# V loaded one group earlier, between two output stores, and one query cast moved from ScalarE to GpSimd

## The chip, the cores and the metric

The kernel runs on one NeuronCore of a Trainium2 chip, as one launch. The metric is the device time of that launch in microseconds. Three runs of the kernel before took 281.1, 279.26 and 280.06 us, a median of 280.06 us. The core has five engines that run side by side: TensorE (PE, matrix products; PEld is its weight load), VectorE (DVE), ScalarE (ACT), GpSimd (POOL) and SyncE (SP), which here only issues DMAs.

## The reference

The computation is an attention with pooled keys and values, followed by a two-layer MLP. There are 8 batches of 8 heads, 576 tokens and a head width of 64.

```python
k_p = k.reshape(B, H, Sp, pool, D).mean(axis=3)      # pool = 8, Sp = 72
v_p = v.reshape(B, H, Sp, pool, D).mean(axis=3)
scores = scale * np.matmul(q, k_p.transpose(0, 1, 3, 2))
attn = softmax(scores)
attn_out = np.matmul(attn, v_p)
x = attn_out.transpose(0, 2, 1, 3).reshape(B * S, H * D)      # 4608 x 512
h = x @ w_in                                                 # 512 -> 2048
out = gelu_tanh(h) @ w_out                                   # 2048 -> 512
```

All inputs and the output are float32. Inside, the kernel works with bf16 operands and float32 sums.

## The kernel before

**Groups.** The 4608 tokens are worked on as nine groups of 512. Groups 0 to 7 take the first 512 tokens of their batch. Group 8, called R, collects the last 64 tokens of all eight batches. The order is `seq = [0, 1, 2, 3, 4, 5, 6, R, 7]`. `n_` counts the place in that order and `g` is the group. While the MLP of one group runs on TensorE, the attention of the next group is prepared on the other engines, and its few products are slipped in between those of the MLP.

**Order by hand.** The scheduler is switched off. The instructions of an engine run in the order in which the program emits them. The MLP of a group (`mlp`, line 536) is a chain of numbered steps, and `at(hooks, s, f, ...)` says that the function `f` is emitted just before step `s`. Steps 0 to 63 are the first layer, steps 64 to 175 are the second (seven products of 16 matmuls each). A step number fixes the place in each engine's queue. It does not fix a time: an engine that has nothing to wait for runs ahead of TensorE. SyncE does this often, and its queue is in order: a DMA whose data or buffer isn't ready holds back all that stand behind it.

**Groups 3 and later are "fast".** Their first layer is `hidden_fast` (line 462), where a part of the products is done with fewer multiplications, out of sums and differences of blocks. Its partial results are `k2`, `k0` and `k1`. `k2` and `k0` are written to two tiles with the tag `osb`, the same two buffers that hold the output rows of the group before until they are stored. Line 500 copies the first product into `k2`, in the buffer of the first store. Line 507 copies the sum `x4` into `k0`, in the buffer of the second. Each has to wait until the store that reads its buffer has landed. After line 507 the product with `S(3)`, at step 28, adds again onto `x4`. The matmuls of these products have line 474, the plain ones of the first layer line 383, those of the second layer line 586.

**Stores.** A group's output leaves in two stores of 512 KB (`store_pair`, line 412): the first after the product 3 (step 159), as soon as VectorE has finished `k0`, the second after the last product (step 175), as soon as ScalarE has copied `x`.

**Loads.** Keys and values of a batch share one tile `kv`, of which there are two buffers, so that batch b uses the buffer of batch b-2. `load_kv(n, parts)` (line 760) makes the tile and issues, on SyncE, the 1 MB of K and two halves of 128 KB (part 0) and the 1 MB of the main part of V (part 1). Lines 112, 107 and 105 are these DMAs; line 121 is the load of the queries (1 MB). Before the change, place `n_` loads the K and V of place `n_ + 2` in one go at step 28 (for `n_ = 1` in two parts, at steps 45 and 164). V of a later group is pooled on VectorE (line 149 and 151) at steps 148 and 161 of the group two places ahead of it, K at steps 5 and 17 of the group one place ahead.

**Transposes.** The cast queries `q_b`, the pooled keys and the exponentials are transposed by DMAs, which SyncE issues too: `qT` (line 232), `kTd` (line 211), `eT` (line 306).

**Query casts.** The queries of group 2 are cast to bf16 by `cast_q` (line 128) in four quarters on ScalarE, at steps 22, 26, 30 and 34 of group 1's MLP. The DMA transpose into `qT` stands at step 35, and the first scores (line 248) at step 68. The queries of later groups are cast by GpSimd.

Of the kernel before, what the change touches and what calls it, by code (L numbers as in the profile page):

```python
# [19 lines left out]
def kernel(  # L20
# [21 lines left out]
    nc = tc.nc  # L42
# [11 lines left out]
    seq = list(range(B - 1)) + [R, B - 1]  # L54
# [33 lines left out]
    st = [dict() for _ in range(B + 1)]  # L88
# [8 lines left out]
    def kv_tile(b):  # L97
        st[b]["kv"] = kvp.tile([128, NB, 8, D], F32, name="kv", tag="kv")
# [4 lines left out]
    def load_half(b, which, eng):  # L103
        if which == "v":
            eng.dma_start(out=st[b]["kv"][64:128, 4], in_=rows(v, b)[0:64])
        else:
            eng.dma_start(out=st[b]["kv"][0:64, 4], in_=rows(k, b)[512:576])

    def load_main(b, which, c0, c1, eng):
        t, w0, b0 = (k, 0, 0) if which == "k" else (v, 64, 5)  # L110
        src = rows(t, b)[w0 + 128 * c0:w0 + 128 * c1].rearrange("(c p) pl d -> p c pl d", p=128)
        eng.dma_start(out=st[b]["kv"][:, b0 + c0:b0 + c1], in_=src)
# [647 lines left out]
    def load_kv(n, parts=(0, 1)):  # L760
        if n != B - 1:
            b = B - 1 if n == R else n
            if 0 in parts:
                kv_tile(b)
                load_main(b, "k", 0, 4, nc.sync)
                load_half(b, "k", nc.sync)
                load_half(b, "v", nc.sync)
            if 1 in parts:
                load_main(b, "v", 0, 4, nc.sync)

    def at(hooks, s, f, *a):
        hooks.setdefault(s, []).append(lambda: f(*a))
# [6 lines left out]
    hooks = {}  # L779
# [46 lines left out]
    for n_, g in enumerate(seq):  # L826
        if n_ == 0:
            continue
        hooks = {}
        fast = n_ >= 3  # L830
        if n_ == 1:
            for i in range(1, 4):
                at(hooks, i, w_sums, i, 0, NP, nc.vector)
            at(hooks, 36, g_sums, 0, 4)
            at(hooks, 57, g_sums, 4, 6, (0,))
        elif fast:
            at(hooks, 41, g_sums, 0, 2, (0,))
            at(hooks, 57, g_sums, 2, 6, (0,))
            at(hooks, 65, g_sums, 6, 8, (0,))
            at(hooks, 65, g_sums, 0, 4, (1,))  # L840
        else:
            at(hooks, 20, g_sums, 0, 2)
            at(hooks, 36, g_sums, 2, 4)
            at(hooks, 57, g_sums, 4, 6, (0,))
        if not fast:
            at(hooks, 65, g_sums, 6, 8, (0,))
        at(hooks, 64 + 32, g_sums, 4, 8, (1,))
        if n_ + 1 < len(seq):
            n = seq[n_ + 1]
            b = B - 1 if n == R else n  # L850
            kv = n != B - 1
            if n_ == 1:
                for j in range(4):
                    at(hooks, 22 + 4 * j, cast_q, n, j, j + 1, nc.scalar)
                at(hooks, 35, qT_tile, n)
                at(hooks, 35, q_transpose_dma, n)
            if kv and not fast:
                t0 = 22 if n_ == 1 else 12
                at(hooks, t0, pool, b, 0, 5)
                at(hooks, t0, dup_k, b, 0, 5)  # L860
                at(hooks, t0, kT_tile, b, None)
                at(hooks, t0, k_transpose_dma, b)
                t1 = t0 + (16 if n_ == 1 else 24)
                at(hooks, t1, pool, b, 5, 9)
                at(hooks, t1, k_spread, b, [nc.gpsimd, nc.gpsimd])
                at(hooks, t1, spread_v, b, nc.gpsimd)
            elif kv:
                at(hooks, 5, pool, b, 0, 5, (0,))
                at(hooks, 17, pool, b, 0, 5, (1,))
                at(hooks, 17, dup_k, b, 0, 5)  # L870
                at(hooks, 17, kT_tile, b, None)
                at(hooks, 17, k_transpose_dma, b)
                at(hooks, 17, spread_gated, b)
                at(hooks, 40, k_spread, b, [nc.gpsimd, nc.gpsimd])
            if fast:
                at(hooks, 2, qT_tile, n)
                at(hooks, 2, q_transpose_dma, n)
            sc_at = [68, 68, 90, 90]
            for j in range(4):
                at(hooks, sc_at[j], scores, n, j)  # L880
                at(hooks, sc_at[j] + 1, exps, n, j)
            at(hooks, 80, eT_tile, n)
            for j in range(4):
                at(hooks, 80 if j < 2 else 92, norm, n, j, nc.vector if j > 1 else nc.gpsimd)
                at(hooks, 80 if j < 2 else 92, e_transpose_dma, n, j)
            at(hooks, 64 + 66, nc.scalar.preload_act_table_set, GELU_SET)
            at(hooks, 64 + 100, xT_tile, n)
            if n_ == 1:
                at(hooks, 64 + 100, values, n, (0,))
                at(hooks, 64 + 107, values, n, (1,))  # L890
            else:
                at(hooks, 64 + 104, values, n)
        if n_ + 2 < len(seq):
            n2 = seq[n_ + 2]
            s2 = 44 if n_ == 1 else 57
            for half, ahead in enumerate((3, 2)):
                if n_ + ahead < len(seq) and seq[n_ + ahead] == R:
                    if half == 0:
                        at(hooks, 9, q_tile, R)
                    at(hooks, 9, gate_queries, g)  # L900
                    at(hooks, 9, load_q, R, 2 * half, 2 * half + 2, nc.gpsimd)
            if n2 != R:
                at(hooks, s2, q_tile, n2)
                at(hooks, s2, load_q, n2, 0, 4, nc.sync)
            at(hooks, 64 + 52, cast_gated, n2)
            if n_ < 2:
                at(hooks, 64 + 100, qT_tile, n2)
                at(hooks, 64 + 100, q_transpose_dma, n2)
                at(hooks, 64 + 100, load_kv, n2, (1,))
            elif n2 != B - 1:  # L910
                b2 = B - 1 if n2 == R else n2
                at(hooks, 64 + 84, pool, b2, 5, 9, (0,))
                at(hooks, 64 + 97, pool, b2, 5, 9, (1,))
            if n_ == 1:
                at(hooks, 45, load_kv, n2, (0,))
            else:
                at(hooks, 28, load_kv, n2)
        mlp(g, hooks, n_ + 1 == len(seq), fast)


# [28 lines left out]
```

## Time and profile before

| | |
|---|---|
| median of three runs | 280.06 us (279.26 to 281.1) |
| the profiled execution | 278.7 us, its span 276.8 us |
| TensorE busy | 268.8 us, 97% |
| VectorE busy | 222.2 us, 80% |
| ScalarE busy | 176.3 us, 64% |
| GpSimd busy | 80.4 us, 29% |
| DMA traffic | 54.37 MB, 196 GB/s on the mean |
| granted TensorE clock | 1.0 throughout |

All times of the trace are counted from the start of the span. The span is the time from the first to the last instruction, and 1.9 us of the profiled execution lie outside it. In the page's second part each digit is the busy share of one fortieth of the span, in tenths, so 9 means 90% or more. In a timeline a row gives the start, the length, the engine, the line and the operation with its output and inputs; a bracket at its end gives how long the engine was idle before it and which instruction or DMA ended that. Matmuls overlap by a little, so that rows of TensorE can run into one another. The chain of waits goes back from the last instruction, at each step to what released it. A row of DMA issues gives how long the transfer took from its issue until it had landed.

The nine groups' MLPs start on TensorE at about 17.7 (group 0), 51.4, 80.2, 109.3, 136.8, 164.7, 192.3 (group 6), 220.5 (R) and 247.9 us (group 7).

### The profile page before, as it was taken

How to read it: one execution, taken by the hardware profiler on the slowest of the kernel's cores; microseconds unless marked ns; L12 is line 12 of the kernel's file. 1: busy time of each engine (PE TensorE's matmuls, PEld its weight loads, DVE VectorE, ACT ScalarE, POOL GpSimd, SP SyncE). 2: the span in 40 equal slices, each digit the busy share in tenths (PEclk: the TensorE clock that was granted, in tenths of full speed). 3: DMA queues.
4: the chain of work that ended last, by engine and by line, in shares of the span. 5: the costliest groups of instructions: out<-in, count | busy, mean ns of one | idle time of the engine just before them, and what ended most of it. 6: DMA issues, size and time to landing. Idle time of an engine off the chain costs nothing.

```text
span 276.8 us, 6558 instructions
## 1 busy us (share of the span) xinstructions
PE 268.8 (97%) x2668; PEld 192.5 (70%) x2686; DVE 222.2 (80%) x365; ACT 176.3 (64%) x265; POOL 80.4 (29%) x122
## 2 busy tenths in 40 slices
PE   8989999999999999999999999999999999999995
PEld 3668844445854588668866876688668966886684
DVE  5886869989966888989998989899989558955832
ACT  1586576579547764696469646964796469646820
POOL 4640282006420532224254425433224200300000
PEclk9999999999999999999999999999999999999999
DMA  7999999998999895899499979964742460253013
GB/s 229 310 195 280 362 385 241 294 366 204 248 215 248 267 278 137 176 300 247 121 216 286 285 134 216 245 184 123 178 154 54 119 152 2 48 117 87 1 41 114
DMA packets 67856, 54.37 MB, mean 196 GB/s; under 512 B 41458, under 2 KB 53746, under 8 KB 67826
## 3 DMA queue, kind: packets, MB, share of 16 engines
q1 hardware_dynamic: 65186, 50.67, 70.7%
q0 software_dynamic: 2496, 3.15, 6.1%
q8 instruction: 21, 0.34, 0.5%
q10 hardware_dynamic: 144, 0.13, 0.1%
q14 instruction: 9, 0.07, 0.1%
HBM read 36.70 MB, written 9.44 MB: 167 GB/s over the span
## 4 chain that ended last, share of the span: by engine, by line
PE 82%; DMA 6%; DVE 6%; ACT 2%; issue 1%; SPq 1%; DVEq 0%; ACTq 0%
PE mm L586 29%; PE mm L383 20%; PE c L474 12%; PE mm L399 5%; PE mm L394 5%; PE xo L344 3%; PE x L586 3%; DMA q_sb<-in_q_dram 2%; PE sc L248 2%; DMA qT<-q_b 2%; DVE den L264 1%; DMA eT<-eb 1%; PE mm L531 1%; DMA out_dram<-osb 1%; DVE eb L279 1%
## 5 line engine op out<-in xcount | busy, mean ns | idle before, releaser
L383 PE MATMUL mm<-xT,w_in_b 128*128 128x512 bf16 x290 | 68.4, 379 | 0.7
L586 PEld LDWEIGHTS <-gT 128*128 128x128 bf16 x512 | 48.3, 98 | 9.0 <-issue 1.4
L385 ACT ACTIVATE gT<-mm 128x512 bf16<-128x512 f32 x76 | 43.6, 599 | 14.3 <-PE mm L383 14.1
L383 PEld LDWEIGHTS <-w_in_b 128*128 128x128 bf16 x304 | 29.7, 98 | 31.0 <-issue 0.5
L586 PEld LDWEIGHTS <-stage 128*128 128x128 bf16 x384 | 37.6, 98 | 4.4
L92 ACT CAST xT<-xo 128x512 bf16<-128x512 f32 (+1 forms) x24 | 13.2, 610 | 28.5 <-PE xo L344 23.9
L586 PE MATMUL mm<-tw,gT 128*128 128x256 bf16 x240 | 30.0, 273 | 0.0
L586 PE MATMUL mm<-w_out_b,gT 128*128 128x256 bf16 x240 | 29.9, 273 | 0.0
L279 POOL TENSOR_TENSOR eb<-e,r 128x576 bf16<-128x576 f32 x14 | 15.8, 1150 | 46.2 <-DVE r L273 24.1
L264 DVE TENSOR_REDUCE den<-e 128x8 f32<-128x576 f32 x36 | 26.2, 729 | 2.9 <-ACT e L257 2.9
L257 ACT ACTIVATE e<-sc 128x576 f32<-128x576 f32 x36 | 22.4, 650 | 7.8 <-POOL eb L279 5.6
L586 PE MATMUL mm<-tw,stage 128*128 128x256 bf16 x224 | 26.7, 273 | 0.0
L92 ACT COPY osb<-mm 128x512 f32<-128x512 f32 x30 | 17.8, 593 | 14.0 <-PE mm L586 13.3
L149 DVE TENSOR_TENSOR kv<-kv 128x1024 f32<-128x1024 f32 (+3 forms) x19 | 23.2, 1220 | 3.8 <-DMA kv<-in_k_dram 2.6
L172 POOL TENSOR_TENSOR vbd<-kvb,vmask 128x256 bf16<-128x256 bf16 (+2 forms) x38 | 22.1, 605 | 5.6 <-DVE kvb L152 4.7
L474 PEld LDWEIGHTS <-ws 128*128 128x128 bf16 x192 | 18.8, 98 | 6.4 <-issue 0.5
L94 POOL CAST q_b<-q_sb 128x1024 bf16<-128x1024 f32 (+1 forms) x15 | 15.5, 1054 | 19.7 <-DMA q_sb<-in_q_dram 19.7
L474 PE MATMUL c<-tt,ws 128*128 128x256 bf16 x144 | 17.7, 272 | 0.1
L279 DVE TENSOR_TENSOR eb<-e,r 128x576 bf16<-128x576 f32 x18 | 17.1, 947 | 0.6
L434 DVE TENSOR_TENSOR stage<-gT 128x512 bf16<-128x512 bf16 (+1 forms) x25 | 13.7, 546 | 4.6 <-ACT gT L385 2.8
L94 POOL COPY kbd<-kTd 64x288 bf16<-64x288 bf16 x12 | 6.4, 533 | 35.0 <-DMA kTd<-kvb 34.7
L435 DVE TENSOR_TENSOR gT<-gT 128x512 bf16<-128x512 bf16 (+1 forms) x25 | 13.2, 528 | 3.4 <-ACT gT L385 1.2
(107 smaller groups left out, 423.6 us busy)
## 6 DMA issues: line engine op xcount, KB each, us to landing
kv<-in_k_dram SPq DMA_DIRECT2D x7, 1024.0 KB, 7.5
q_sb<-in_q_dram SPq DMA_DIRECT2D x7, 1024.0 KB, 9.9
kv<-in_v_dram SPq DMA_DIRECT2D x6, 1024.0 KB, 9.2
out_dram<-osb SPq DMA_DIRECT2D x12, 512.0 KB, 3.1
out_dram<-osb SPq DMA_DIRECT2D x11, 256.0 KB, 3.4
kv<-in_v_dram SPq DMA_DIRECT2D x4, 512.0 KB, 9.9
w_in_b<-in_moe_w_in_dram POOLq DMA_DIRECT2D x4, 512.0 KB, 6.8
w_out_s<-in_moe_w_out_dram SPq DMA_DIRECT2D x2, 1024.0 KB, 13.7
```

The source lines that it names most:

```text
L92: eng.copy(out=out, in_=in_)
L94: eng.tensor_copy(out=out, in_=in_)
L149: add(out=t[:, :, 0:4, :], in0=t[:, :, 0:4, :], in1=t[:, :, 4:8, :], op=ALU.add)
L172: eng.tensor_tensor(out=vbd[p0:128, b, n0:n1, :].rearrange("p (c r) (hh d) -> p c (r hh) d", c=max(m, 1), d=D), in0=kvb[p0:128, 4 + c0:4 + ...
L257: nc.scalar.activation(out=e.rearrange("p (x h) s -> p x (h s)", x=2), in_=sc[:, :, 0:4 * Sp], func=ACT.Exp, scale=1.0 / 64.0)
L264: nc.vector.reduce_sum(out=den, in_=e, axis=AX.X)
L279: eng.tensor_tensor(out=o.rearrange("p (pr hh s) -> p hh pr s", hh=2, s=Sp), in0=e.rearrange("p (hh pr) s -> p hh pr s", hh=2), in1=r.rear ...
L383: nc.tensor.matmul(out=hp, lhsT=w_in_b[:, ko, fo * 128:(fo + 1) * 128], rhs=st[g]["xT"][:, ko, :], start=(i == 0), stop=(i == KO - 1))
L385: nc.scalar.activation(out=gT[:, fo, :], in_=hp, func=ACT.Gelu_apprx_tanh)
L394: nc.tensor.matmul(out=hp[:, f, :], lhsT=w_in_b[:, ko, (fo + f) * 128:(fo + f + 1) * 128], rhs=st[g]["xT"][:, ko, c0:c0 + 256], start=(ko ...
L474: nc.tensor.matmul(out=acc[:, m, :], lhsT=lhs(i, m), rhs=rhs(i), start=bool(fresh and i == 0 and m % 2 == 0), stop=(i == 1), skip_group_ch ...
L586: nc.tensor.matmul(out=xs[p] if acc is xs else acc[:, p, :], lhsT=lt, rhs=rt, start=bool(fresh and m == 0 and (p == 0 or (last and acc is ...
```

## The change

Two things are moved.

First, V. In places `n_ = 2` and later, step 28 now loads only K and the two halves of place `n_ + 2`. The V of place `n_ + 3` is loaded at step 175 of place `n_`, between the first and the second output store. This happens at the ends of groups 2, 3 and 4, for the V of batches 5, 6 and 7. The V of batch 4, for which there is no earlier place, is loaded at step 14 of group 2, ahead of its K. As V can now be the first to use the tile, `load_kv` makes the tile when it isn't there yet.

Second, the last quarter of group 2's queries is cast by GpSimd at step 22. The other three stay on ScalarE at steps 22, 26 and 30.

```diff
     def load_kv(n, parts=(0, 1)):
         if n != B - 1:
             b = B - 1 if n == R else n
+            if "kv" not in st[b]:
+                kv_tile(b)
             if 0 in parts:
-                kv_tile(b)
                 load_main(b, "k", 0, 4, nc.sync)
                 load_half(b, "k", nc.sync)
                 load_half(b, "v", nc.sync)
...
             if n_ == 1:
                 for j in range(4):
-                    at(hooks, 22 + 4 * j, cast_q, n, j, j + 1, nc.scalar)
+                    at(hooks, 22 + 4 * (j % 3), cast_q, n, j, j + 1, nc.gpsimd if j == 3 else nc.scalar)
...
-            if n_ == 1:
-                at(hooks, 45, load_kv, n2, (0,))
-            else:
-                at(hooks, 28, load_kv, n2)
+            at(hooks, 45 if n_ == 1 else 28, load_kv, n2, (0,))
+            if n_ == 2:
+                at(hooks, 14, load_kv, n2, (1,))
+            if n_ > 1 and n_ + 3 < len(seq):
+                at(hooks, 64 + 111, load_kv, seq[n_ + 3], (1,))
         mlp(g, hooks, n_ + 1 == len(seq), fast)
```

## The prediction

> **What bounds the kernel now.** I read the page's busy times and slices first, then the chain of waits in order of time, then the timelines of the queues that the change touches.
>
> ```profile
> PE 268.8 (97%) x2668; PEld 192.5 (70%) x2686; DVE 222.2 (80%) x365; ACT 176.3 (64%) x265; POOL 80.4 (29%) x122
> PE   8989999999999999999999999999999999999995
> ```
>
> TensorE is busy in every slice. Between 20 and 273 us it has hardly a gap, so a gain can come only out of the few gaps left, while every stall of PE adds its full length. The two gaps that the change can reach are this one, before the first scores of group 2 (PE timeline; the bracket is idle time and its cause):
>
> ```profile
> 66.42 0.46 PE L248 MATMUL sc<-kbd,qT 64*64 64x72 bf16 x32 [0.38 <-DMA qT<-q_b]
> ```
>
> and 0.28 us in group 4: its stretch, from first matmul to first matmul (136.82 to 164.65), is 27.83 us where group 3's is 27.55, and the chain shows its values waiting for the last eT transpose, 3.7 us in flight.
>
> Now SyncE's queue around the end of group 2, in order of issue (start, time on the queue):
>
> ```profile
> 107.55 3.00 SPq L415 DMA_DIRECT2D out_dram<-osb  x2
> 110.65 3.74 SPq L232 DMA_TRANSPOSE qT<-q_b  x1
> ...
> 116.65 0.57 SPq L112 DMA_DIRECT2D kv<-in_k_dram  x1
> ...
> 118.47 0.59 SPq L112 DMA_DIRECT2D kv<-in_v_dram  x1
> ```
>
> The two output stores go out at 107.55 and 110.21. The next group's L507, ScalarE's copy of x4 into k0, writes the second store's buffer, so it waits for that store to land. ScalarE's timeline for groups 3, 4 and 5:
>
> ```profile
> 114.17 1.01 ACT L507 COPY osb<-c 128x1024 f32<-128x1024 f32 x1 [0.79 <-DMA out_dram<-osb]
> 141.25 1.01 ACT L507 COPY osb<-c 128x1024 f32<-128x1024 f32 x1 [0.32 <-PE c L474]
> 169.07 1.01 ACT L507 COPY osb<-c 128x1024 f32<-128x1024 f32 x1 [0.32 <-PE c L474]
> ```
>
> Behind L507 stands PE: the product with S(3) adds onto x4 and may start only when the copy has read it. The chain of waits shows those starts, and at the last boundary, where a late store already sets the pace, how fast PE follows (start, length, what):
>
> ```profile
> 115.36 0.91 PE c L474 x8
> ...
> 142.91 0.87 PE c L474 x8
> ...
> 170.73 0.87 PE c L474 x8
> ...
> 249.48 3.47 DMA out_dram<-osb
> 253.05 1.02 ACT osb L507
> 254.11 1.03 PE c L474 x8
> ```
>
> PE starts 1.06 us after L507 does. So L507 must start by 114.30, 141.85 and 169.67 (S(3) start less 1.06), or PE stalls. The second stores were issued at 110.21, 137.76 and 165.58; the last two landed 3.0 and 3.1 us later, at 140.76 and 168.68, the first let L507 go at 114.17. The slack is 0.13, 1.09 and 0.99 us.
>
> **What the Trainium skill says.** "DMA: Bandwidth & Descriptors", Queues, rings and completion order: transfers issued from SyncE share one row of rings, and each DMA engine consumes descriptors in ring order. So a load issued between two stores is served before the second. The trace agrees in the one place where this already happens, the end of group 1: V is issued at 82.06 and the store at 82.72, and that store took (DMA issues of 82 to 84 us; KB each, us to landing)
>
> ```profile
> out_dram<-osb SPq DMA_DIRECT2D x1, 512.0 KB, 9.1
> ```
>
> instead of about 3. "GPSIMD Engine Reference", Specifications: GpSimd shares its SBUF interfaces with VectorE, which contends where an operation has two SBUF inputs. The trace agrees: the 128x1024 add of L149 took 1.67 us at 105.25, next to a GpSimd cast, and 1.22 us at 63.03 without.
>
> **The change, part by part.**
>
> V between the stores (groups 5, 6 and 7's V, at the ends of groups 2, 3 and 4). One 1 MB load of 0.57-0.59 us of queue time goes after store 0, at about 107.90, 135.55 and 163.14 (store 0's issue plus its 0.36). It doesn't hold back the issue of store 1, which comes at 110.21, 137.76 and 165.58 after ScalarE's copy. What it holds back is that store's data. The data rate at the end of group 2, 108 to 112 us in 40 slices of 0.1 us:
>
> ```profile
> DMA  0001997997999979508000000000005899899797
> GB/s 0 0 0 41 492 410 328 492 451 328 451 410 410 410 328 492 205 0 164 0 0 0 0 0 0 0 0 0 0 0 246 328 532 369 328 451 410 328 410 328
> ```
>
> Store 0's data end at 109.9, store 1's begin at 111.0, and between them the engines are idle for 1.1 us. The same look at the next two boundaries gives 137.3 and 138.6, 164.9 and 166.4. V fits partly into these holes. Its time: group R's Q load, 1 MB with nothing behind it (issued at 199.64), moved at about 375 GB/s between 201.6 and 204.4, so 1.05 MB takes 2.8 us; counted with its slow ends it was 3.3 us. I take 3.0. V's data then run from 109.9 to 112.9, 137.3 to 140.3 and 164.9 to 167.9, and store 1 starts 1.9, 1.7 and 1.5 us later than now. Taking off the slack leaves PE stalls of 1.77, 0.61 and 0.51 us: **+2.9 us**. With 2.8 us it is 2.3, with 3.3 us 3.8. Nothing hides a stall, as PE has no other gap in which to make it up. If the 0.9 us by which the first store lands slower than the other two (3.9 against 3.0) is taken up in the delay, the low end is 1.4. ScalarE itself, late by the slack on top, has 0.97 us idle before the gelu at 144.68 to catch up.
>
> Behind store 1 on SyncE are the qT transposes and, after VectorE's dup, the kT transpose. qT lands 1.5 to 1.9 us later (5.0 to 5.6 us after issue now), around 118, and the scores come at 122.83: free. If that cover of 5 us were gone the delay would be PE's.
>
> V no longer loaded at step 28. In groups 3 and 4 the burst there loses 1 of 3.25 MB, 2.8 us of DMA time, and Q lands earlier. In group 4 Q landed 11.8 us after its issue at 147.09, at 158.9, just where the last eT transpose starts; without V it ends near 156, the transpose takes the usual 2.6-2.7 us instead of 3.7, and PE's 0.28 us go: **-0.28 us**, bounded by 0. Other groups had no such wait. In group 5 V leaves a burst without a Q load: 0.
>
> Group 4's own V, moved from after to before K in group 2 (step 14 against 28): SyncE runs ahead of the steps, and K was issued at 85.93 right behind the kT transpose, so only the order of the two loads changes. K is needed at the first add of group 3, 110.52, V at 105.25; both land before 101: 0.
>
> The cast. ScalarE casts group 2's four quarters at 57.80, 58.82, 59.82 and 60.81 (0.62 us each); the qT transpose is issued at 61.47, right after. With the fourth on GpSimd, idle until 64.68, q_b is ready at 60.44. A 128x512 cast on GpSimd took 0.62 (w_out) to 0.87 us (q), so it ends before 58.8. SyncE is held by the kT transpose from 59.60 to 60.82, so qT goes at about 60.87, 0.6 earlier, lands 4.9 us later at 65.8, and PE wants it at 66.04. The 0.38 us gap goes: **-0.38 us**. It is less if the cast slows VectorE's add at 57.86 (two SBUF inputs, at most 0.45 us, by the L149 pair above): kT is then issued by 60.05 and qT at 61.27, a gain of 0.2; and if the transposes are held by the backlog of loads that drains near 62.3, zero. ScalarE's 0.62 us saved is off the path.
>
> **Sum.** 2.9 - 0.28 - 0.38 = +2.2 us. Against the profiled execution: 278.7 us (span 276.8 and 1.9 around it) becomes 280.9. That execution lies 1.4 below the median of the runs, 280.06; the same difference on the median gives **282.3**.
>
> **The rivals.**
> - The holes swallow V (faster). If V starts while store 0 still drains and the engines reach the 450-490 GB/s of single slices, V needs 2.2 us, and the longer landing of the first store is absorbed: no stall, and the two gains remain: 280.06 - 0.66 = 279.4. For it: 1.1 to 1.5 us of hole plus about 1 us of slack at two boundaries. Against: slack of 0.13 at the first, and no load in the trace held more than about 400.
> - Store behind load lands late (slower). At the end of group 1 V landed at 89.26 (7.2 us) and the store 2.5 us after it, at 91.8, although its data take 1.4. If this repeats, V ends at 113.2, 140.6 and 168.2 (3.3 us), lands 0.65 later (as Q did) and the stores come at 116.35, 143.75 and 171.35: stalls of 2.05, 1.9 and 1.7, together 5.6, less 0.4 of gains: 285.3. It decides once the stores land over 5 us after their issue. Against: there the transposes and the K and Q loads crowded the queue, here nothing follows but qT.
> - The load doesn't go where it says: its buffer isn't free and it waits. The buffer of group 3's V was last read at 92.3, 15 us before; the next ones 20 us before. Then the times stay, with the cast alone: 279.7.
>
> **How the numbers follow.** Forecast 0.64, holes 0.14, late stores 0.19, not as said 0.03. The likeliest case alone runs from +0.7 (1.4 - 0.66) to +3.8 (no gain): 280.8 to 283.9. To leave out no more than 2 in 10 the range goes half-way into both rivals: 279.5 to 284.7. One per cent, 2.8 us, is about what a measurement of this kernel can tell from no change. Slower by more: the late stores and a quarter of the forecast, 0.36. Faster by more would need gaps that PE doesn't have: 0.03. The rest, 0.61, is within.
>
> **What would show it.** Right: V's issue next to store 0 on SyncE; store 1 landing 4.5 to 5.5 us after issue; L507 waiting for the store for over 1 us in groups 3, 4 and 5, then a gap of PE before the S(3) product, longest in group 3; no gap at 66 and none at the end of group 4. Wrong: L507 still released by PE in groups 4 and 5 (the holes), or PE gaps of 2 us in each (late stores), or a new gap of PE elsewhere, at the values or the scores.

## The result, and the profile after

The changed kernel took 289.02 us, the median of six runs from 287.41 to 290.63. The kernel before took 279.73 us in six runs beside them. The ratio is 1.0324, with a 95% interval from 1.0276 to 1.0373: slower by 9.3 us, where 2.2 were forecast and 284.7 us was the end of the range. Here and below the times are medians of all runs of a kernel, while the ratios leave out the few runs marked as slow, so that the two can differ a little. The profiled execution took 288.41 us with a span of 286.7 us, 9.9 us more than the span before.

The page's busy times, and the slices of TensorE and of its clock:

```profile
PE 271.6 (95%) x2686; PEld 192.9 (67%) x2686; DVE 222.1 (77%) x365; ACT 175.3 (61%) x264; POOL 80.1 (28%) x123
...
PE   7889999999999999599969997999999999999995
...
PEclk9999999999999999999999999799999999999999
```

There are three dips of TensorE now, in groups 3, 4 and 5, and one slice in which its clock was not granted in full. The other engines did the same work as before, but for the one cast that moved.

SyncE's queue at the end of group 2 (start, time on the queue) shows that V went where the diff puts it, behind the first store and ahead of the second:

```profile
108.14 0.35 SPq L415 DMA_DIRECT2D out_dram<-osb  x1
108.55 0.42 SPq L112 DMA_DIRECT2D kv<-in_v_dram  x1
110.92 0.36 SPq L415 DMA_DIRECT2D out_dram<-osb  x1
111.38 6.42 SPq L232 DMA_TRANSPOSE qT<-q_b  x1
```

ScalarE's line 507 in groups 3, 4 and 5 now waits 3 to 4 us for the store at all three places:

```profile
118.18 1.01 ACT L507 COPY osb<-c 128x1024 f32<-128x1024 f32 x1 [4.09 <-DMA out_dram<-osb]
...
148.24 1.01 ACT L507 COPY osb<-c 128x1024 f32<-128x1024 f32 x1 [3.36 <-DMA out_dram<-osb]
...
178.03 1.01 ACT L507 COPY osb<-c 128x1024 f32<-128x1024 f32 x1 [3.00 <-DMA out_dram<-osb]
```

And TensorE waits for line 507 with the product S(3), 7.7 us in all:

```profile
119.24 1.03 PE L474 MATMUL c<-tt,ws 128*128 128x256 bf16 x8 [3.17 <-ACT osb L507]
...
149.30 1.03 PE L474 MATMUL c<-tt,ws 128*128 128x256 bf16 x8 [2.44 <-ACT osb L507]
...
179.09 1.87 PE L474 MATMUL c<-tt,ws 128*128 128x256 bf16 x8 [2.09 <-ACT osb L507]
```

The last of these rows is also longer: its eight matmuls took 1.87 us instead of 1.03. Busy time by stretch around it (stretch, its length, busy time of PE, PEld, DVE, ACT and POOL, granted clock, DMA share, GB/s) says why:

```profile
177.00:179.00 2.00, 0.00 (x1) 0.00 (x0) 1.14 (x2) 0.97 (x2) 1.86 (x5) 1.00 1.26 234
179.00:183.00 4.00, 3.91 (x17) 2.27 (x17) 1.23 (x1) 1.81 (x4) 1.97 (x4) 0.57 1.12 160
183.00:187.00 4.00, 4.00 (x26) 2.36 (x25) 3.15 (x5) 3.79 (x6) 0.84 (x2) 1.00 1.08 338
```

After the gap TensorE ran at about half its clock, and only got it back near 182.5. The four matmuls of line 383 behind S(3) took 1.88 us instead of 1.03, so this costs 1.7 us on top of the gap.

The sum for the profiled execution goes by the groups' first matmul of line 474. Group 3 took 30.79 us (27.55 before), group 4 30.15 (27.82), group 5 31.34 (27.62). That is 3.24, 2.33 and 3.72 us more. Group 3 began 0.71 us later (109.82 against 109.11), and from group 6 on the stretches are as before. Together 10.0 us, which is the span's 9.9.

### The profile page after: what moved, and what is told of

It is laid out like the page before. It is cut to its first block, busy times and chain, and to the rows that moved or that the text cites. A ratio compares the mean times of both kernels' runs of the same rounds, so it can differ in the third digit from the quotient of the medians.

```text
span 286.7 us, 6575 instructions
## 1 busy us (share of the span) xinstructions
PE 271.6 (95%) x2686; PEld 192.9 (67%) x2686; DVE 222.1 (77%) x365; ACT 175.3 (61%) x264; POOL 80.1 (28%) x123
## 4 chain that ended last, share of the span: by engine, by line
PE 75%; DMA 16%; DVE 4%; ACT 3%; issue 1%; SPq 1%; POOL 0%; ACTq 0%; DVEq 0%
PE mm L586 30%; PE mm L383 19%; PE c L474 10%; DMA out_dram<-osb 7%; PE mm L399 5%; DMA w_out_s<-in_moe_w_out_dram 5%; PE x L586 2%; PE xo L344 2%; PE sc L248 2%; DMA q_sb<-in_q_dram 2%; DMA qT<-q_b 2%; PE mm L531 1%; ACT xT L92 1%; PE mm L394 1%; ACT osb L507 1%
## 5 line engine op out<-in xcount | busy, mean ns | idle before, releaser
L383 PE MATMUL mm<-xT,w_in_b 128*128 128x512 bf16 x304 | 71.0, 382 | 0.0
L474 PE MATMUL c<-tt,ws 128*128 128x256 bf16 x144 | 18.5, 280 | 7.7 <-ACT osb L507 7.7
L94 POOL CAST q_b<-q_sb 128x1024 bf16<-128x1024 f32 (+1 forms) x16 | 16.1, 1026 | 30.0 <-DMA q_sb<-in_q_dram 30.0
L394 PE MATMUL mm<-xT,w_in_b 128*128 128x256 bf16 x128 | 15.6, 273 | 0.1
```

The costliest lines, as they stand in the source:

```text
L94: eng.tensor_copy(out=out, in_=in_)
L383: nc.tensor.matmul(out=hp, lhsT=w_in_b[:, ko, fo * 128:(fo + 1) * 128], rhs=st[g]["xT"][:, ko, :], start=(i == 0), stop=(i == KO - 1))
L394: nc.tensor.matmul(out=hp[:, f, :], lhsT=w_in_b[:, ko, (fo + f) * 128:(fo + f + 1) * 128], rhs=st[g]["xT"][:, ko, c0:c0 + 256], start=(ko ...
L474: nc.tensor.matmul(out=acc[:, m, :], lhsT=lhs(i, m), rhs=rhs(i), start=bool(fresh and i == 0 and m % 2 == 0), stop=(i == 1), skip_group_ch ...
```

## The experiments

Two parts of the change were first taken alone.

**The cast alone.** The diff against the kernel before:

```diff
-                    at(hooks, 22 + 4 * j, cast_q, n, j, j + 1, nc.scalar)
+                    at(hooks, 22 + 4 * (j % 3), cast_q, n, j, j + 1, nc.gpsimd if j == 3 else nc.scalar)
```

> The kernel before with only the cast moved. Theory A (the loss is the V load ahead of the second store): within 0.5 us of before, since the kT transpose on SyncE and VectorE's slowed add keep the qT transpose where it was, so PE's gap at the scores of group 2 stays between 0.3 and 0.7 us. Rival B (a good part of the loss is the cast: a late kT or qT pushes everything): 2 us or more slower.

It took 279.29 us, ratio 0.9993 (0.9971 to 1.0015). TensorE's gap at the scores of group 2 stayed:

```profile
66.83 0.45 PE L248 MATMUL sc<-kbd,qT 64*64 64x72 bf16 x32 [0.49 <-DMA qT<-q_b]
```

Part of the reason stands on VectorE and SyncE. The add of line 151 ran next to GpSimd's cast and took 1.11 us, where the kernel before had 0.82 (the add, and then the transposes behind it):

```profile
58.43 1.11 DVE L151 TENSOR_TENSOR kv<-kv 128x640 f32<-128x640 f32 x1
```

```profile
60.47 1.22 SPq L211 DMA_TRANSPOSE kTd<-kvb  x1
61.85 3.08 SPq L232 DMA_TRANSPOSE qT<-q_b  x1
```

This execution began group 1 some 0.58 us later (51.92 us against 51.34). Counted from there kT was issued 0.29 us later than before (60.47 against 59.60) and qT, held behind it, only 0.2 us earlier (61.85 against 61.47), while TensorE came to the scores 0.28 us earlier, and so the gap did not close. In the time of the kernel no gain and no loss can be seen.

**V alone.** The changed kernel with that line put back.

> The changed kernel with the cast back on ScalarE. Theory A: 9 us slower than before, like the changed kernel, with the same three gaps of PE behind line 507, 7 to 8 us together. Rival B: at most 7 us slower.

It took 288.68 us, ratio 1.0281 (1.0205 to 1.0357), and so the loss is V's, as far as these runs can tell. Its profiled execution happened to be the fastest of its runs, at 284.91 us: the gaps behind line 507 were 6.1 us together, and the clock was granted in full. In it TensorE also waited once, for 0.6 us, at the scores of group 5 for GpSimd's `kbd` copy, which needs the kT transpose. The three others had a mean clock of 0.987 to 0.994 and took 288.3 to 289.4 us.

**V behind the second store.**

```diff
-            if n_ > 1 and n_ + 3 < len(seq):
-                at(hooks, 64 + 111, load_kv, seq[n_ + 3], (1,))
+            if n_ > 2 and n_ + 2 < len(seq):
+                at(hooks, 0, load_kv, n2, (1,))
```

> The changed kernel with the same three V loads issued right behind the second store instead of in front of it. Theory A (order in SyncE's rings): the stores land in 3 to 4 us again, line 507 no longer stalls PE, time within 1 us of before. Rival C (the load at this place slows the boundary whatever its order, by sharing engines and memory with the store): the second stores land 5 us or later and the time stays 4 us or more above before.

This was a miss for both: 293.38 us, ratio 1.0475 (1.042 to 1.0529), slower than the change itself. The gaps behind line 507 did go, as theory A says, and the stores landed in time. Another wait took their place, TensorE's longest now (who waited for whom, us in total, times, longest):

```profile
PE sc L248 <- POOL kbd L94: 10.0, 5, 5.1
```

GpSimd's `kbd` copies wait for kT. The chain of waits has the transposes of groups 4 and 5:

```profile
146.90 8.84 DMA kTd<-kvb
...
179.68 10.63 DMA kTd<-kvb
```

Before the change kT was issued at 142.94 and 170.77, and took 2.6 to 5.8 us where a landing was seen. With V in front, the qT transpose sits on SyncE's queue for 5.5 to 7.3 us instead of 3.2 to 3.7, kT is issued later behind it, and lands late behind it too. So the queue behind the second store has no room for V either; the cover of 5 us that the prediction gave to qT is not there for kT.

**The wait behind V taken away.** Here V stays in front of the store, but `k0` no longer uses the store's buffer:

```diff
-        k2, k0, k1 = part(), part(), spare
+        k2, k0, k1 = part(), stage[:, 2048:3072].rearrange("p (m t) -> p m t", m=4), spare
```

> The changed kernel with k0 written into the idle third of the sums' buffer instead of the second store's buffer, so that line 507 has no store to wait for. V stays in front of the store. Theory A: PE's three gaps go, the store still lands 6 to 7 us after its issue, time within 1 us of before. Rival D (a late qT or another wait behind V is next in line): a new gap of PE, time 3 us or more above before.

It took 282.29 us, ratio 1.0103 (1.005 to 1.0156). The gaps behind line 507 are gone while the stores at the first and third place still land 6.9 and 5.9 us after their issue. The wait of line 507 for the store, with the clock that it costs, is therefore about 6.5 of the 9.3 us. Some 2.8 us are left, more than theory A allowed and a little less than rival D. In the profiled execution (280.87 us) two other waits stand for part of that:

```profile
PE xo L344 <- DMA eT<-eb: 1.3, 1, 1.3
...
PE sc L248 <- POOL kbd L94: 1.0, 2, 0.6
```

The second hangs on a kT transpose behind V. The first doesn't: the four eT transposes were on SyncE's queue from 127.30 to 133.24 us, ahead of the V of that boundary (135.50). What caused that wait stays open.

Four runs then asked why the store comes later than forecast.

**qT moved away from behind the store.**

```diff
-                at(hooks, 2, qT_tile, n)
-                at(hooks, 2, q_transpose_dma, n)
+                at(hooks, 17 if kv else 2, qT_tile, n)
+                at(hooks, 17 if kv else 2, q_transpose_dma, n)
```

> The changed kernel with the qT transpose of groups 4, 5, 6 and R's predecessors (all fast places that have keys to pool) taken from right behind the second store and put behind the kT transpose, some 6 us later. V stays in front of the store. Theory F (the store lands at 6 to 7 us because the transpose queued right behind it is served at the same time and takes engine time from V and the store): stores land 4.5 to 5 us after issue, PE's three gaps shrink from 7.7 to 2 to 4 us, time 3 to 5 us above before. Rival G (a 1 MB load in this place takes 7 us whatever follows it): stores still land 6 us or later, time 8 to 10 us above before.

It took 288.94 us, ratio 1.032 (1.0241 to 1.0399). Theory F falls: with nothing queued behind them for 5 us, the stores still landed after 6.9, 6.6 and 6.3 us, and the gaps were about as long as with qT in its place, 7.8 us together:

```profile
118.55 1.03 PE L474 MATMUL c<-tt,ws 128*128 128x256 bf16 x8 [2.92 <-ACT osb L507]
150.46 1.83 PE L474 MATMUL c<-tt,ws 128*128 128x256 bf16 x8 [2.56 <-ACT osb L507]
182.02 1.03 PE L474 MATMUL c<-tt,ws 128*128 128x256 bf16 x8 [2.27 <-ACT osb L507]
```

**Half of V.** `load_kv` gets two more parts, the halves of V's main part. The first stands where V stood, the second is back at step 28.

```diff
-            if 1 in parts:
-                load_main(b, "v", 0, 4, nc.sync)
+            for p, c0, c1 in ((1, 0, 4), (2, 0, 2), (3, 2, 4)):
+                if p in parts:
+                    load_main(b, "v", c0, c1, nc.sync)
...
-            at(hooks, 45 if n_ == 1 else 28, load_kv, n2, (0,))
+            at(hooks, 45 if n_ == 1 else 28, load_kv, n2, (0, 3) if n_ > 2 else (0,))
...
-                at(hooks, 64 + 111, load_kv, seq[n_ + 3], (1,))
+                at(hooks, 64 + 111, load_kv, seq[n_ + 3], (2,))
```

> The changed kernel with half of V (512 KB) in front of the second store and the other half back at step 28. Theory A with the order of the rings and a cost by bytes: the store lands about 1.7 us earlier than with all of V, at 4.5 to 5.3 us; gaps of PE 1.3 to 1.7 us at the first boundary and under 0.8 at the two others, together under 3 us and no half-clock stretch; time 1 to 3 us above before. Rival H (any load in front of the store costs the full delay, by latency and not by bytes): 6 us or more above before.

It took 280.9 us, ratio 1.0059 (1.0041 to 1.0078), inside the 1 to 3 us of theory A, and rival H falls. But the cost falls faster than the bytes: half of them cost about 1.7 us where all of them cost 9.3. The half landed 4.2 to 4.5 us after its issue, the stores behind it 4.2 us after at the first place and 3.6 at the third (3.9 and 3.1 before), sooner than the 4.5 to 5.3 us of theory A, and the one gap left in the profiled execution is

```profile
115.32 1.03 PE L474 MATMUL c<-tt,ws 128*128 128x256 bf16 x8 [0.25 <-ACT osb L507]
```

That execution, at 278.98 us, was the fastest of its 20 runs, so the rest of the 1.7 us is not seen in it.

**V in front of both stores.**

```diff
-                at(hooks, 64 + 111, load_kv, seq[n_ + 3], (1,))
+                at(hooks, 64 + 56, load_kv, seq[n_ + 3], (1,))
```

> The changed kernel with the same V loads one place further ahead, in front of the first store and behind the eT transposes, when the DMA engines are idle. Theory A: V is through before the second store is issued, which lands in 3 to 4 us; the first store lands about 1 us later, which line 500 can take; time within 1 us of before. Rival D (V near the boundary delays whatever transfers follow it): gaps of PE behind line 500 or 507 of over 1 us each, time 3 us or more above before.

A miss for theory A: 285.42 us, ratio 1.023 (1.0133 to 1.0327). V was issued 1.6 to 2.6 us ahead of the first store and had not left the engines when that came. The first store landed 4.9 to 5.7 us after its issue, and line 500, which waits for it, held TensorE, as rival D has it, for less than its 1 us only at the first place:

```profile
113.64 1.03 PE L474 MATMUL c<-tt,ws 128*128 128x256 bf16 x8 [0.82 <-ACT osb L500]
...
143.55 1.03 PE L474 MATMUL c<-tt,ws 128*128 128x256 bf16 x8 [1.56 <-ACT osb L500]
...
173.73 1.03 PE L474 MATMUL c<-tt,ws 128*128 128x256 bf16 x8 [1.66 <-ACT osb L500]
```

**V with nothing behind it.** On top of the moved `k0` and the moved qT, the second store of groups 2, 3 and 4 is put off to step 17 of the next group.

```diff
+                if g in (2, 3, 4):
+                    late.append(lambda: store_pair(g, 1, osb[1]))
+                else:
+                    store_pair(g, 1, osb[1])
-                store_pair(g, 1, osb[1])
...
+        if late:
+            at(hooks, 17, late.pop())
         mlp(g, hooks, n_ + 1 == len(seq), fast)
```

> The changed kernel with k0 in the sums' buffer, the qT transpose behind kT, and the second store of groups 2, 3 and 4 put off to behind both (step 17 of the next group, which nothing waits for now). So V follows the first store with nothing behind it on SyncE for some 6 us. Theory S (V is slowed to 7 us because the second store is served next to it): V lands 6.3 us or less after its issue, that is the 5.6 us of the lone Q load and the 0.7 us for which the first store's data still run. Rival G (a lone 1 MB load behind a store takes that long): V still lands at 6.8 us or later. Time of the whole kernel: within 1 us of before where PE has no gap left; up to 3 us above if scores wait for the late transposes.

It took 281.66 us, ratio 1.006 (1.0024 to 1.0096). V landed 6.2, 7.5 and 7.1 us after its issue; in the changed kernel it was 7.5, 7.4 and 6.9. At the first place V was 1.3 us faster than there, one execution against one. At the two others V is as slow alone, which is rival G. The data rate of the second place (134 to 146 us in 40 slices of 0.3 us):

```profile
DMA  4200049999498396999999700000056378497999
GB/s 84 55 0 0 0 137 382 396 382 314 157 225 68 27 184 253 403 382 335 403 430 382 260 21 27 20 27 27 0 123 191 123 123 205 164 235 224 218 152 285
```

The store's data end at about 137. The load begins at a low rate, runs at 335 to 430 GB/s for 1.8 us, and ends in five slices at 20 to 27 GB/s. The transfer has landed only when those last slices are through. In them a single one of the 16 DMA engines is still at work (141.05 to 142.46 us; packets, MB, share of 16 engines):

```profile
q1 hardware_dynamic: 18, 0.03, 6.4%
```

One sixteenth is 6.25%. At the third place about three engines were left for the last 1.1 us (20.8%), and at the first there is no such tail. So this load landed with its slowest engine. Why an engine falls behind isn't settled. A 16 KB load of instructions kept one engine busy for 1.2 us from 134.6 us on, but the trace doesn't say whether it was the same one; GpSimd's loads of R's queries are issued in groups 4 and 5 as well, and they were not tried apart.

**`k0` moved in the kernel before.** The line of the fourth experiment, without the change.

> The kernel before with only k0 moved to the sums' buffer. Theory A: line 507 waits for no store at any boundary, PE's 0.2 us gap at the last boundary (store of R ahead of group 7) goes; 0 to 0.4 us faster than before, too little to tell from no change. Rival: the buffer of the sums brings a wait of its own, 1 us or more slower.

It took 279.26 us, ratio 0.9982 (0.9959 to 1.0005): not to be told from no change. No version was found that clearly beats the kernel before. Its gaps leave under 1 us to win.

## Why the prediction was wrong

**The chain was right.** V is served ahead of the second store, the store lands late, line 507 waits for it and S(3) for line 507, longest in group 3. The order shows in the packets: each of these transfers closes with sixteen packets of 4 bytes, and the first of V's and the first data of the second store both stand at 114.02 us (at 144.72 and 175.30 at the other places). The fourth run, which takes away only the wait of line 507 for the store, gives back about 6.5 of the 9.3 us.

**The step that failed is the size of V's time.** The prediction took 3.0 us of data for V, from the Q load that lands 5.6 us after its issue. In the changed kernel V landed 7.5, 7.4 and 6.9 us after. Its packets can be told from the stores' in the trace by their size, 2 KB against 4 KB: they ran for 5.1, 5.0 and 4.7 us, at the first place from 110.5 to 115.6. Put into the prediction's sum in place of 3.0, these make stalls of 3.87, 2.61 and 2.21 us, 8.7 together, where 7.7 were measured. The data rate at the first place (108 to 118 us in 40 slices of 0.25 us) shows two slow stretches, one from 110.25 to 111.25 and one from 112.25 to 113.5:

```profile
DMA  0001999899591678979977999999999992328409
GB/s 0 0 0 49 426 393 360 328 328 213 180 172 25 238 303 328 254 238 197 213 197 254 344 369 418 442 385 475 434 312 284 242 138 98 138 74 94 29 18 215
```

So the second stores landed 7.2, 6.4 and 6.1 us after issue instead of 4.5 to 5.5, and the gaps were 3.17, 2.44 and 2.09 us instead of 1.77, 0.61 and 0.51. A single row was taken as the price of a load, and it was the fastest of its kind: K and V loads of 1 MB were seen to land 5.7 to 11.3 us after their issue in the profile before. The upper bound of 3.3 us was that same row counted more widely, and therefore no bound; the Q load's own packets ran for 3.7 us. Why V's data take longer stays open. The store behind V is not needed for it: at the second and third place of the run with nothing behind V they took 5.2 and 4.6 us, at the first 3.6.

**A term was missing: TensorE's clock.** The Trainium skill, "TensorE: Matmul & The Clock Gate", Part 1, has a monitor halve the clock of an idle TensorE, in free-running windows of 3.4 us, and gives as a rule no idle gap of more than about 3.4 us. In this trace the clock was halved after a gap of 2.09 us and not after one of 3.17. The half-clock stretch lasted 3.41 us and cost 1.7. On the length of the gap the measurement differs from the page; on the windows it agrees. In the run with the moved qT the half-clock stretches begin at 119.81 and 150.53 us, 9 times 3.413 us apart, in the run with V behind the store at 156.33 and 190.46 us, 10 times. Each profile's first rise of the clock lies on the same grid: 4.98 us in the changed kernel, 51 times 3.413 us ahead of the half-clock stretch at 179.06. Three windows of that grid in the changed kernel, and the stretch after the last (columns as above):

```profile
114.21:117.62 3.41, 1.86 (x14) 1.13 (x12) 2.93 (x5) 0.00 (x0) 1.25 (x4) 1.00 1.25 236
117.62:121.03 3.41, 1.79 (x13) 1.21 (x13) 0.66 (x1) 2.46 (x3) 1.44 (x3) 1.00 1.14 199
...
175.65:179.06 3.41, 1.35 (x9) 0.69 (x7) 2.42 (x4) 1.03 (x2) 3.27 (x7) 1.00 1.23 311
179.06:182.47 3.41, 3.38 (x13) 1.79 (x13) 1.23 (x1) 1.42 (x2) 1.91 (x4) 0.50 1.02 143
```

The gap of 3.17 us falls into two windows, 1.55 and 1.62 us into each, and the clock stays. The gap of 2.09 us falls almost whole into one, 2.06 us, and the clock is halved for the next. Over groups 3 to 5 of the profiles of this case, the clock fell after each of the six windows in which TensorE was idle for 1.90 us or more, and after none with 1.85 or less. One of the six, in the run with nothing behind V, holds only two shorter gaps, of 1.25 and 0.65 us. So it is not the gap's length alone that counts, but how much of it one window holds. (A single window at the very end of the kernel before, idle for 1.91 us, did without a fall, so the border is not exact.)

The six runs of the changed kernel had a mean clock of 0.982 to 0.994. One stretch makes 0.006 of it, so each of them had one to three, an estimate of about 1.7 to 5 us. The kernel before had next to no gap, and so the question wasn't asked.

**The rival of the late stores** came nearest, with stalls of 5.6 us and 285.3 us in all. Its landings (6.1, 6.0 and 5.8 us after issue) are short of the measured ones by 0.3 to 1.1 us, and it lacks the clock. The range was cut off half-way to it.

**The holes did not swallow V**, though they all but swallowed half of it, and the load did go where the code puts it.

**The cast** was forecast at -0.38 us, with 0.2 and zero as bounds. The whole kernel shows no gain, and its interval (0.8 us faster to 0.4 slower) can't tell zero from the 0.2. VectorE's add was slowed by 0.3 us, within the 0.45 us named, and qT stayed behind kT. The gap itself is not steady either: the profiled execution with V alone, whose casts are as before, has none at these scores.

**Group 4's -0.28 us** is borne out in kind, by 0.11 us: no eT wait of TensorE is left at that place, and group 4 is 2.33 us longer where its gap alone is 2.44.

**What qT's delay would cost** was set at nothing. For the change as it stands no gap at the scores of groups 4 to 6 came of it. But the third run shows kT next in line, at up to 5.1 us a place, and the second and fourth have waits of up to 0.6 us for it.

## What to carry to other kernels

A load in front of a store on the same queue holds the store back, here by 3.0 to 3.4 us for 1 MB, and the next writer of the store's buffer pays for it. Before moving a transfer into a hole of the DMA's time, follow each later transfer of that queue to who waits for it, and take the load's price from the slow end of the rows seen, not from the one that ran alone. On a TensorE that has had no gaps, count with each new gap of about 2 us or more the chance of a slower clock after it.

## What the runs showed of the hardware that wasn't expected

A 1 MB load behind a store, with nothing queued behind it on SyncE, landed only after 6.2 to 7.5 us. At one of three places its last 1.4 us were the work of a single DMA engine out of 16, at about a sixteenth of the rate. Half of the bytes landed after 4.2 to 4.5 us. A qT transpose behind such a load and its store held SyncE's queue for 5.4 to 6.4 us instead of 3.2 to 3.7, and the next transposes with it. TensorE's clock fell to half for 3.41 us after a gap as short as 2.09 us and stayed full after one of 3.17: what these runs go by is the idle time inside one window of a fixed grid of 3.41 us, with the border near 1.9 us.
